# Rounding of the parameters at two points of a step, with temporaries of their own, and the mask placed ahead of a maximum of the next step

## The chip, the cores and the metric

The kernel runs on one core of a Trainium2 chip. Its time is the device time in microseconds (us) of one execution. Before the change the median of three executions is 1976.49 us (1976.48 to 1977.78). The profile is of one more execution, which took 1976.97 us.

## The reference, cut to what matters

```python
# attention: q, k, v are (8, 8, 576, 64)
scores = scale * q @ k.T
kth  = the 32nd largest score of each row
attn = softmax of the scores >= kth, 0 elsewhere
x    = (attn @ v), laid out as (8, 576, 512)
# mixer: U is (576, 32), V (32, 576), w_ch1 (512, 2048), w_ch2 (2048, 512)
u    = x + (x^T @ U @ V)^T
out  = u + relu(u @ w_ch1) @ w_ch2
```

The four mixer parameters arrive as 64-bit numbers. The kernel has to turn each into a rounded 32-bit one itself; the text calls this the rounding.

## The kernel before, in words

**Steps.** Two heads make a pair, four pairs a batch, and there are 32 pairs. A pair's 576 rows are cut into five row tiles, t = 0 to 4. The main loop (L528) runs one step for each row tile, n = 5 * pair + t, 160 steps and two more to drain. Steps with t = 0 to 3 are long (128 rows of two heads, so two chunks of 128x576 scores); those with t = 4 are short (64 rows of each head in one chunk). Twenty steps are one batch.

**What a step issues, in program order.** PE (TensorE) and ACT (ScalarE) work in exactly this order; DVE (VectorE), POOL (GpSimd) and SP (the DMA queue) are ordered by a scheduler.

1. The loads of the next pair on SP (t = 0), and the first maximum of each chunk of step n, on DVE (`first`, L292).
2. Calls of `fill()`, each of which may advance the `mixed` generator and emit a portion of the MLP, with the rest of the transposes of step n-2 between them (`turns`, L334 and L339 on PE, L335 and L340 on ACT) and one transpose of the next pair's q, k (`prep`, L228).
3. `values(n-2)` (L364, L367 or L354) and `scores(n+1)` (L247 on PE, then the copies L265 to L267 or L257 on ACT).
4. The second part of `front(n)`: ACT makes `nmax` (L294) and the exponential of chunk 0 (L272); DVE makes three rounds of match_replace and max for each chunk (L299, L303); for chunk 1 POOL builds the mask from the 32nd value and adds it to the scores (L305, L306); for chunk 0 DVE masks the exponential and sums it (scalar_tensor_tensor, L307, "the mask").
5. Two calls of `fill`, the first transposes of step n-1 (L334), two more calls, and then the exponential of chunk 1 of step n-1 on ACT (L272), which reads what POOL left. Its transposes come first thing in step n+1.
6. `next_params` (L559).

**The MLP.** The MLP of batch b goes into the twenty steps after the batch, in portions of four matmuls: portions of `u @ w_ch1` (L437), each followed by a relu on ACT into a tile `hT` (L447), and portions of `h @ w_ch2` (L454). Every fourth of the latter ends with a sum on DVE (`oT`, L467), whose transposes (L479) and output DMA are emitted with a later portion. `due` is a budget in portions: each `fill` adds `share` in a long step and `SHORT * share` in a short one, and portions are emitted while it is above zero. `mixed(g)` makes `u` for a pair: a transpose of XT (L388), a scaling on DVE (`x`, L390), `pT` (L401), and twice `up` (L413, L415) with its copy to `uT` (L422). The MLP of the first batch is emitted from step 22 on, and that of the last runs behind the loop.

**The rounding.** There are 36 parameter pieces, most of 128x512. `next_params(n)` does three things in this order: it joins every piece that is under way, it splits every piece that was loaded, and it starts n loads. A split is Abs and a conversion of one byte on ACT (L141, L143) with a maximum on POOL between (L142); a join is two bit operations on DVE (L149, L152) and an addition on POOL (L156). `next_params` is called at the end of each step, with 2 in steps 0 and 1, 1 in steps 2 to 17 and 2 from then on. The temporaries `bits` and `low` are taken from the ten buffers of `hT`, two for each piece, five pieces deep; raw pieces have three buffers. `uT`, where u^T of a batch is built, has two buffers of 128x2304, of which the second is first used by batch 1.

Of the kernel before, what the change touches and what calls it, by code (L numbers as in the profile page):

```python
# [8 lines left out]
F32 = mybir.dt.float32  # L9
U8 = mybir.dt.uint8  # L10
U32 = mybir.dt.uint32
# [10 lines left out]
def kernel(  # L22
# [28 lines left out]
    nc = tc.nc  # L51
    B, H, S, D = q.shape
    P = 128
# [3 lines left out]
    NF, NC = F // P, C // P  # L57
# [8 lines left out]
    HT = 10  # L66
# [6 lines left out]
    mlpp = ctx.enter_context(tc.tile_pool(name="mlpp", bufs=2))  # L73
# [9 lines left out]
    WIDE = 2 * P + TAIL  # L83
# [33 lines left out]
    def half(h):  # L117
        return slice(h * D, (h + 1) * D)


    def f64_raw(srcs):


        n, w = srcs[0].shape[0], srcs[0].shape[1]
        raw = mlpp.tile([P, 2 * C], U32, tag="raw", name="raw", bufs=3)[:, 0:w]
        for i, src in enumerate(srcs):
            nc.sync.dma_start(raw[i * n : (i + 1) * n], src)
        return raw[0 : len(srcs) * n]

    def f64_parts(raw):  # L130


        n, w = raw.shape[0], raw.shape[1] // 2
        hi = raw.rearrange("p (w two) -> p w two", two=2)[:, :, 1]
        low8 = raw.bitcast(U8).rearrange("p (w eight) -> p w eight", eight=8)[:, :, 3]
        bits, low = (
            mlpp.tile([P, 2, WIDE], U32, tag="hT", name=name, bufs=HT)
            .rearrange("p a n -> p (a n)")[0:n, 0:w]
            for name in ("bits", "low")
        )  # L140
        nc.scalar.activation(bits.bitcast(F32), hi.bitcast(F32), AF.Abs)  # L141
        nc.gpsimd.tensor_scalar(bits.bitcast(F32), bits.bitcast(F32), TINY, None, ALU.max)  # L142
        nc.scalar.activation(low, low8, AF.Identity, bias=half_bit[0:n], scale=1.0 / 32)  # L143
        return hi, bits, low

    def f64_join(hi, bits, low, outs):


        nc.vector.tensor_scalar(  # L149
            bits, bits, 3, 0x3FFFFFFF, ALU.logical_shift_left, ALU.bitwise_and  # L150
        )
        nc.vector.scalar_tensor_tensor(  # L152
            out=bits, in0=hi, scalar=0xC0000000, in1=bits, op0=ALU.bitwise_and, op1=ALU.bitwise_or
        )
        for dst, form in outs:
            nc.gpsimd.tensor_tensor(dst.bitcast(U32), form(bits), form(low), ALU.add)  # L156

    SLAB = 512

    def same(a):  # L160
        return a
# [9 lines left out]
    for cc in range(NC):  # L171
        for f in range(0, F, SLAB):
            params.append(
                ([moe_w_ch1[cc * P:(cc + 1) * P, 2 * f:2 * (f + SLAB)]], [(w1[:, cc, f:f + SLAB], same)])
            )
# [5 lines left out]
    def next_params(n):  # L181

        while parts:
            f64_join(*parts.pop(0))
        while raws:
            r, outs = raws.pop(0)
            parts.append((*f64_parts(r), outs))
        for _ in range(min(n, len(params))):
            srcs, outs = params.pop()
            raws.append((f64_raw(srcs), outs))  # L190


    raw, qkTs, S2s, uTs, XTs, dens = {}, {}, {}, {}, {}, {}
    probs, PTs = {}, {}

    def load(g):
        b, h0 = g // NPAIR, 2 * (g % NPAIR)
        tiles = []
        ends = loads.tile([P, 2, D], F32, tag="ld_ends", name="ld_ends")
        for name, src in (("q", q), ("k", k)):  # L200
            t = loads.tile([P, NT, 2, D], F32, tag=f"ld_{name}", name=f"ld_{name}")
            for i in range(2):
                nc.sync.dma_start(
                    t[:, :, i, :],
                    src[b, h0 + i, 0:MAIN, :].rearrange("(p t) d -> p t d", t=NT),
                )
            nc.sync.dma_start(
                ends[half(len(tiles))], src[b, h0 : h0 + 2, MAIN:S, :].rearrange("h p d -> p h d")
            )
            tiles.append(t)  # L210
        va, vd, vt = (a[g % NV] for a in (vas, vds, vts))
        for i in range(2):
            nc.sync.dma_start(
                va[:, i], v[b, h0 + i, 0:MAIN, :].rearrange("(p t) d -> p t d", t=NT)
            )
            nc.sync.dma_start(vd[half(i), half(i)], v[b, h0 + i, MAIN:S, :])
        nc.sync.dma_start(vt[TAIL:P], v[b, h0 : h0 + 2, MAIN:S, :].rearrange("h p d -> p h d"))
        raw[g] = tiles, ends
# [51 lines left out]
    def weigh(chunk, E, nmax, total=None):  # L270

        nc.scalar.activation(E, chunk, AF.Exp, bias=nmax, scale=SCALE, accum_out=total)  # L272

    def front(g, t):

        if t == 0:
            dens[g] = small.tile([P, 2 * NT + 1], F32, tag="den", name="den", bufs=3)
        chunks, den = S2s.pop((g, t)), dens[g]  # L280
        n = len(chunks)
        E2 = attn.tile([P, 2 * S], F32, tag="E", name="E", bufs=3)
        Es = [E2[:, c * S : (c + 1) * S] for c in range(n)]
        sums = [den[:, 2 * t + c : 2 * t + c + 1] for c in range(n)]
        probs[g, t] = E2
        curs, ms = list(chunks), [None] * n
        first = small.tile([P, 2, 8], F32, tag="first", name="first", bufs=3)
        nmax = small.tile([P, 2], F32, tag="nmax", name="nmax", bufs=4)
        order = (1, 0) if n == 2 else (0,)
        for c in order:  # L290
            ms[c] = first[:, c]
            nc.vector.max(ms[c], curs[c])  # L292
        yield
        nc.scalar.mul(nmax[:, 0:n], first[:, 0:n, 0], -SCALE)  # L294
        weigh(chunks[0], Es[0], nmax[:, 0:1])
        for i in range(1, TOPK // 8):
            for c in order:
                nxt = attn.tile([P, S], F32, tag="rr", name="rr", bufs=3)
                nc.vector.match_replace(nxt, ms[c], curs[c], NEG)  # L299
                curs[c] = nxt  # L300
            for c in order:
                ms[c] = small.tile([P, 8], F32, tag="m8", name="m8", bufs=8)
                nc.vector.max(ms[c], curs[c])  # L303
        if n == 2:
            nc.gpsimd.tensor_scalar(Es[1], chunks[1], ms[1][:, 7:8], NEG, ALU.is_lt, ALU.mult)  # L305
            nc.gpsimd.tensor_tensor(chunks[1], chunks[1], Es[1], ALU.add)  # L306
        nc.vector.scalar_tensor_tensor(  # L307
            out=Es[0],
            in0=chunks[0],
            scalar=ms[0][:, 7:8],  # L310
            in1=Es[0],
            op0=ALU.is_ge,
            op1=ALU.mult,
            accum_out=sums[0],
        )
        if t == NT:
            del qkTs[g]
        yield
        if n == 2:
            weigh(chunks[1], Es[1], nmax[:, 1:2], sums[1])  # L320
        yield
# [174 lines left out]

    CH = NT + 1
    STEPS = NP * CH
    SLOTS, SHORT = 8, 0.55
    share = MLP_WORK / (NPAIR * SLOTS * (NT + SHORT))  # L500
    fillers, mixing, due = [], [], 0.0

    def fill(n=1):

        nonlocal due
        for _ in range(n):
            if mixing and next(mixing[0], True):
                mixing.pop(0)
            due += share * (SHORT if t == NT else 1)
            while due > 0:  # L510
                if not fillers:
                    due = 0.0
                    break
                done = next(fillers[0], None)
                if done is None:
                    fillers.pop(0)
                else:
                    due -= done

    load(0)  # L520
    next_params(2)
    t = 0
    for _ in prep(0):
        pass
# [3 lines left out]
    for n in range(STEPS + 2):  # L528
        g, t = divmod(n, CH)
        if n < STEPS:  # L530
            if t == 0 and g + 1 < NP:
                load(g + 1)
            if t == 1 and g + 1 < NP:
                ready = prep(g + 1)
            fronts[n] = front(g, t)
            next(fronts[n])
        fill()
        next(turning, None)
        fill()
        next(turning, None)  # L540
        fill()
        next(ready, None)
        fill()
        if n >= 2:
            values(*divmod(n - 2, CH))
        if n + 1 < STEPS:
            scores(*divmod(n + 1, CH))
        if n < STEPS:
            next(fronts[n])
        if n >= 2 and (n - 2) % CH == NT:  # L550
            mixing.append(mixed((n - 2) // CH))
        fill(2)
        if 1 <= n <= STEPS:
            turning = turns(*divmod(n - 1, CH))
        next(turning, None)
        fill(2)
        if 1 <= n <= STEPS:
            next(fronts.pop(n - 1))
        next_params(1 if 2 <= n < 18 else 2)  # L559
    while mixing or fillers:  # L560
        fill()

# [30 lines left out]
```

## Time and profile before

| what | value |
|---|---|
| median of three executions | 1976.49 us |
| profiled execution | 1976.97 us |
| its span, first to last instruction | 1975.2 us |
| PE busy | 1797.4 us (91%) |
| DVE busy | 1640.3 us (83%) |
| ACT busy | 950.5 us (48%) |
| POOL busy | 574.7 us (29%) |
| mean TensorE clock granted | 0.955 of full speed |

Busy time is what the instructions of an engine cover. An idle time stands with the group of instructions that it comes before, and with the engine that ended it. The matmul rows count each float32 matmul twice, since the chip makes two passes, so a portion of four matmuls is a row "x8". The page's second part cuts the span into 40 slices of 49.4 us.

### The profile page before, as it was taken

The page shows a single profiled execution, that of the slowest core. Times are in us where ns is not written, and L with a number is a line of the kernel's source. Part 1 is how long each engine was busy: PE and PEld are TensorE (multiplying, and loading weights), DVE is VectorE, ACT ScalarE, POOL GpSimd, SP SyncE. Part 2 cuts the span into 40 slices and gives each one's busy share as a digit, 9 for nine tenths or more (in the row PEclk, how much of TensorE's full clock was granted, in tenths as well). Part 3 has the DMA queues.
Part 4 walks back from the last instruction along what each step waited for, and adds up shares of the span by engine and source line. Part 5 has one row for each costly group of instructions (what it writes and reads, how often), then busy time and mean ns, then how long its engine had stood idle before and what let it go on. Part 6 is the DMA issues. An engine that isn't in the chain of part 4 may idle for free.

```text
span 1975.2 us, 29361 instructions
## 1 busy us (share of the span) xinstructions
PE 1797.4 (91%) x10656; PEld 1361.2 (69%) x10656; DVE 1640.3 (83%) x3433; ACT 950.5 (48%) x2345; POOL 574.7 (29%) x346
## 2 busy tenths in 40 slices
PE   4666678999999999999999999999999999999999
PEld 2444455777667876677666876677776876678777
DVE  7899998889898988989899888989898898988000
ACT  4555565454554545454554545445454545454111
POOL 4545564222222322222232232222232222223000
PEclk7757689999999999999999999999999999999999
DMA  4212231100001010000101010101001000000000
GB/s 102 72 56 73 66 94 44 29 18 24 15 22 30 19 29 20 24 23 14 25 22 30 20 29 14 26 15 25 24 20 30 22 25 20 15 7 4 8 14 11
DMA packets 121151, 58.22 MB, mean 29 GB/s; under 512 B 89904, under 2 KB 116784, under 8 KB 121008
## 3 DMA queue, kind: packets, MB, share of 16 engines
q1 hardware_dynamic: 121008, 56.36, 10.7%
q8 instruction: 84, 1.38, 0.3%
q14 instruction: 59, 0.48, 0.1%
HBM read 46.89 MB, written 9.44 MB: 29 GB/s over the span
## 4 chain that ended last, share of the span: by engine, by line
PE 75%; DVE 14%; ACT 7%; issue 2%; DMA 1%; POOL 1%; SPq 0%; ACTq 0%; DVEq 0%; POOLq 0%
PE mm L437 24%; PE mm L454 21%; PE sc L247 8%; PE O L367 6%; DVE rr L299 5%; PE tp L334 5%; DVE m L303 5%; ACT E L272 2%; PE O L354 2%; PE up L413 2%; PE up L415 2%; PE O L364 2%; PE tp L228 1%; DVE first L292 1%; DVE E L307 1%
## 5 line engine op out<-in xcount | busy, mean ns | idle before, releaser
L303 DVE MAX8 m<-rr 128x8 f32<-128x576 f32 x864 | 614.7, 747 | 3.6 <-DVE rr L299 0.5
L305 POOL TENSOR_SCALAR E<-Ssb,m 128x576 f32<-128x576 f32 x128 | 284.8, 2225 | 1109.3 <-DVE m L303 728.6
L437 PE MATMUL mm<-uT,w 128*128 128x256 f32 (+1 forms) x2048 | 539.2, 409 | 0.0
L454 PE MATMUL mm<-hT,w 128*128 128x256 f32 (+1 forms) x2048 | 537.1, 408 | 0.0
L437 PEld LDWEIGHTS mm<-uT,w 128*128 128x128 f32 x2048 | 372.3, 190 | 109.3 <-issue 21.9
L454 PEld LDWEIGHTS mm<-hT,w 128*128 128x128 f32 x2048 | 372.1, 190 | 102.0 <-issue 16.6
L299 DVE MATCH_REPLACE8 rr<-m,rr 128x576 f32<-128x576 f32 x576 | 427.7, 743 | 0.0
L292 DVE MAX8 first<-Ssb 128x8 f32<-128x576 f32 x288 | 211.2, 751 | 162.1 <-ACT Ssb L267 160.2
L334 PE MATMUL tp<-ident,E 128*128 128x128 f32 x1152 | 187.3, 287 | 97.2 <-ACT E L272 73.1
L334 PEld LDWEIGHTS tp<-ident,E 128*128 128x128 f32 x1152 | 140.8, 146 | 163.6 <-ACT E L272 95.0
L447 ACT ACTIVATE hT<-mm 128x320 f32<-128x320 f32 (+1 forms) x256 | 105.1, 411 | 273.3 <-PE mm L437 265.5
L335 ACT COPY PT<-tp 128x512 f32<-128x512 f32 x288 | 168.0, 583 | 122.7 <-PE tp L334 119.4
L272 ACT ACTIVATE E<-Ssb,nmax 128x576 f32<-128x576 f32 x288 | 223.3, 775 | 6.9 <-POOL Ssb L306 1.6
L247 PE MATMUL sc<-qkT 64*128 64x288 f32 (+1 forms) x1280 | 212.7, 454 | 0.7 <-ACT qkT L229 0.5
L299 DVE MATCH_REPLACE8 rr<-first,Ssb 128x576 f32<-128x576 f32 x288 | 212.2, 742 | 0.0
L306 POOL TENSOR_TENSOR Ssb<-Ssb,E 128x576 f32<-128x576 f32 x128 | 192.2, 1501 | 10.7
L367 PE MATMUL O<-PT,va 128*64 128x128 f32 x2048 | 151.5, 294 | 0.0
L247 PEld LDWEIGHTS sc<-qkT 64*128 64x128 f32 (+1 forms) x1280 | 111.0, 189 | 52.6 <-issue 26.2
L467 DVE TENSOR_TENSOR oT<-uT,mm 128x320 f32<-128x320 f32 (+1 forms) x64 | 28.3, 442 | 139.2 <-PE mm L454 139.2
L307 DVE SCALAR_TENSOR_TENSOR E<-Ssb,m,E 128x576 f32<-128x576 f32 x160 | 134.0, 838 | 2.5 <-ACT E L272 1.5
L367 PEld LDWEIGHTS O<-PT,va 128*64 128x64 f32 x2048 | 118.6, 145 | 16.9 <-issue 3.1
L376 ACT COPY XT<-O 128x128 f32<-128x128 f32 x128 | 34.1, 267 | 176.5 <-PE O L367 176.5
(64 smaller groups left out, 1426.9 us busy)
## 6 DMA issues: line engine op xcount, KB each, us to landing
raw<-in_moe_w_ch_dram SPq DMA_DIRECT2D x32, 512.0 KB, 3.8
ld_q<-in_q_dram SPq DMA_DIRECT2D x64, 128.0 KB, 2.8
ld_k<-in_k_dram SPq DMA_DIRECT2D x64, 128.0 KB, 2.8
va<-in_v_dram SPq DMA_DIRECT2D x64, 128.0 KB, 2.4
out_dram<-ob SPq DMA_DIRECT2D x64, 128.0 KB, 1.9
ld_ends<-in_q_dram SPq DMA_DIRECT2D x32, 32.0 KB, 2.1
ld_ends<-in_k_dram SPq DMA_DIRECT2D x32, 32.0 KB, 2.1
vd<-in_v_dram SPq DMA_DIRECT2D x64, 16.0 KB, 1.9
```

Source lines behind the costliest of these rows:

```text
L247: nc.tensor.matmul(sc[slice(0, n) if t < NT else half(h), h, 0:HALF], lhsT=qkT[half(h), 0, cols(t)], rhs=qkT[half(h), 1, i * HALF : (i + 1 ...
L272: nc.scalar.activation(E, chunk, AF.Exp, bias=nmax, scale=SCALE, accum_out=total)
L292: nc.vector.max(ms[c], curs[c])
L299: nc.vector.match_replace(nxt, ms[c], curs[c], NEG)
L303: nc.vector.max(ms[c], curs[c])
L305: nc.gpsimd.tensor_scalar(Es[1], chunks[1], ms[1][:, 7:8], NEG, ALU.is_lt, ALU.mult)
L306: nc.gpsimd.tensor_tensor(chunks[1], chunks[1], Es[1], ALU.add)
L334: nc.tensor.transpose(tp[:, j, :], E2[:, a : a + P], ident)
L335: nc.scalar.copy(PT[:, NT * h : NT * h + NT], tp)
L367: nc.tensor.matmul(O[half(h)], lhsT=va[:, h, j, :], rhs=PT[:, NT * h + j], start=False, stop=(j == NT - 1),)
L437: nc.tensor.matmul(ph[:, 0:w], lhsT=w1[:, cc, f * P : (f + 1) * P], rhs=uT[:, cc, lo:hi], start=(cc == 0), stop=(cc == NC - 1),)
L454: nc.tensor.matmul(po[:, 0:w], lhsT=w2[:, f, c * P : (c + 1) * P], rhs=hTs[f][:, 0:w], start=(f == 0), stop=(f == NF - 1),)
```

## The change

Five edits:

- The temporaries of the rounding are four slabs of 128x512 in one `uT` tile that is allocated ahead of all others, so that it takes one of the two buffers. Pieces use the slabs in turn, two slabs each, so two pieces can be under way.
- `next_params(1)` is also called in the middle of each step, between the two `fill` calls ahead of the transposes of step n-1. The call at the end of the step starts one load in even steps and none in odd ones, and the first call, ahead of the loop, starts one in place of two.
- The first of the maxima that step n+1 issues (chunk 1 in long steps) may not stand ahead of the mask of step n on DVE. It is an order in the instruction stream and no semaphore.
- SHORT goes from 0.55 to 0.65, which also lowers `share`.
- `SLAB` is defined further up.

```diff
-        bits, low = (
-            mlpp.tile([P, 2, WIDE], U32, tag="hT", name=name, bufs=HT)
-            .rearrange("p a n -> p (a n)")[0:n, 0:w]
-            for name in ("bits", "low")
-        )
+        if not spare:
+            uT = mlpp.tile([P, NC, S], F32, tag="uT", name="uT")
+            words = uT.rearrange("p c n -> p (c n)").bitcast(U32)
+            spare.extend(words[:, i * SLAB : (i + 1) * SLAB] for i in range(4))
+        bits, low = (spare.pop(0) for _ in range(2))
+        spare.extend((bits, low))
+        bits, low = bits[0:n, 0:w], low[0:n, 0:w]
...
-            nc.vector.max(ms[c], curs[c])
+            ins = nc.vector.max(ms[c], curs[c])
+            if last_mask:
+                tc.add_manual_dep(ins.ins, last_mask.pop(), mybir.DependencyInfo(
+                    mybir.DependencyClass.NoSync, mybir.DependencyReason.DATA
+                ), reason="order")
...
-        nc.vector.scalar_tensor_tensor(
+        ins = nc.vector.scalar_tensor_tensor(
...
+        last_mask.append(ins.ins.name)
...
-    SLOTS, SHORT = 8, 0.55
+    SLOTS, SHORT = 8, 0.65
...
-    next_params(2)
+    next_params(1)
...
-        fill(2)
+        fill()
+        next_params(1)
+        fill()
...
-        next_params(1 if 2 <= n < 18 else 2)
+        next_params((n + 1) % 2)
```

More of the change, by code (lines that the diff above doesn't have):

```diff
@@ L118, in half @@
         return slice(h * D, (h + 1) * D)
+    SLAB = 512
+    spare = []
     def f64_raw(srcs):
@@ L156, in f64_join @@
             nc.gpsimd.tensor_tensor(dst.bitcast(U32), form(bits), form(low), ALU.add)
-    SLAB = 512
     def same(a):
@@ L193 @@
     raw, qkTs, S2s, uTs, XTs, dens = {}, {}, {}, {}, {}, {}
-    probs, PTs = {}, {}
+    probs, PTs, last_mask = {}, {}, []
     def load(g):
```

## The prediction, made before the changed kernel was run

> **What bounds the kernel now.** I read the busy digits first (page, second part).
>
> ```profile
> PE   4666678999999999999999999999999999999999
> ...
> DVE  7899998889898988989899888989898898988000
> ```
>
> For seven slices (some 340 us) PE is half idle while DVE is nearly full; then PE is full, and for the last three DVE has nothing. The steps give the exact borders: step 19's mask starts at 236.55, step 28's score matmuls at 336.56, the last scores end at about 1811. The table by stage (length, then busy us by engine, PE first, DVE third; then the clock granted), its third row one batch:
>
> ```profile
> 11.50:236.55 225.05, 138.97 (x755) 96.41 (x757) 216.12 (x457) 121.18 (x281) 118.72 (x81) 0.67 0.26 72
> 236.55:336.56 100.01, 75.44 (x414) 53.38 (x412) 95.48 (x195) 54.32 (x124) 61.32 (x40) 0.87 0.24 73
> ...
> 470.07:695.06 224.99, 216.33 (x1334) 164.88 (x1332) 200.57 (x420) 113.57 (x284) 59.68 (x32) 1.00 0.09 23
> ```
>
> So up to about 337 us DVE is the bound (96% and 95% busy), from there PE (96%), each batch of twenty steps taking 225.0 us, and the end (163.8 us) is MLP on PE, 158.5 us of it busy. All roundings (L149, last at 322.4) lie in the DVE part. What can be won there is DVE's idle time, in this view of DVE's waits up to 340 us (total, times, longest):
>
> ```profile
> DVE first L292 <- ACT Ssb L267: 17.5, 4, 10.7
> DVE x L390 <- PE tp L388: 6.6, 3, 3.6
> DVE bits L149 <- POOL bits L142: 1.7, 2, 1.5
> ```
>
> 10.65 us of the first row is the wait for the first scores. The rest is 15.2 us: 1.46, 0.75 and 4.65 for scores, 2.04, 3.59 and 0.96 for x, 1.7 for POOL. Up to step 28's first maximum (338.70) DVE's work is the same in both kernels, so what the opening wins or loses is the change of these 15.2 us. In the PE part the gain is in PE's waits of one batch, 8.6 us in all:
>
> ```profile
> PE tp L334 <- ACT E L272: 5.1, 6, 1.3
> ...
> PE tp L479 <- DVE oT L467: 0.7, 1, 0.7
> ```
>
> **The change part by part.** I set the instruction orders of both built programs side by side.
>
> *Rounding twice a step.* It removes and adds no instruction; it starts 1.5 pieces a step throughout. In DVE's order 31 pieces are joined by step 19's mask, where 22 were; all by step 23's, where it was step 27's. Nine joins at 0.42 + 0.68 (L149, L152 undisturbed) move 9.9 us of DVE work ahead of step 19's mask and out of the steps behind it. By itself that is neutral: both sides are DVE's. What it takes away is idle: the hT buffers are no longer lent out. Before, a relu stood 6.8 us behind a join of w (the only L447 wait on POOL), which is what made scores 28 late: the 4.65 us. ACT's four waits for raw pieces (11.0 and 5.2 us) should go too: a raw buffer is freed by the join three pieces earlier, two steps back at 1.5 a step, one and a half at 2. They cost DVE nothing now, as PE and ACT catch up; SP has the same loads, spread out.
>
> *What it adds.* The join now often stands on DVE in the step of its split. Abs waits for the POOL addition of two pieces before (two pieces of slabs), with ACT's copies for the transposes queued behind it; that addition is half a step old, so I cost this at nothing (its ends: 0, and 1.6, the one such wait of before). DVE's first bit operation waits for POOL's maximum, which stands behind POOL's L305 and L306. In step 8 of before these ended at 119.25, 2.3 us after the mask (116.92). In the changed short steps 9 and 19, two joins stand among seven rounds. The first is 4 rounds (2.7 us at 0.667 each, the start-to-start distance of its rounds) behind the mask; its input is ready at 2.3 + 1.3 (addition) + 1.5 (maximum) = 5.1. The second waits 1.5 more. That is 4 us in each of steps 9 and 19, and 1.5 in 4 and 14 by the same count: 11 us. From below it is nothing: before, such waits sum to 1.7 us over 36 joins, and POOL's spans are rough. I take 7, nearer the computed row.
>
> *Mask ahead of the next maximum.* In the order of the changed program one of the two maxima still stands ahead of most masks; the other follows. In the opening this puts step 4's, 9's and 14's mask three rounds (2 us) earlier against the work of the next step, so x, which needs that mask through PE, comes due later on DVE: of the waits for x I keep 1.4 + 0.7 + 1.4 (step 5, 10, 15) in place of 2.04 + 3.59 + 0. The other waits for scores and x (1.46, 0.75, 0.96, 4.65) I count as gone, since PE and ACT no longer stand behind raw pieces and hT, and the 1.7 is replaced by the 7. So idle after is 3.5 + 7 = 10.5, against 15.2: **-4.7**, with ends 3.5 (-11.7) and 14.5 plus up to 3 where PE, at S(28), is as late as DVE (+2.3).
>
> In the PE part, DVE idles 22.6 us a batch waiting for scores, and there the mask now waits for ACT's exponential, which ACT does after the copies: 642.22 first maximum, exponential over at 643.10, mask, second maximum, against two maxima and the mask. DVE goes on 0.3 us later in eight steps of a batch, 0.7 in some; the next wait (1.2 to 4.4 us) takes it back. It shows only where PE waits for DVE: x at step 57 has 0.3 us of room (I take 0.1, ends 0 and 0.3, times 7: +0.7), and oT of step 41, now one maximum (0.67) earlier: 0.4 less of its 0.73 wait, six times: **-2.4**, ends -4.4 and 0.
>
> *SHORT.* Portions shift in four steps of twenty. In 17 one goes behind a transpose (no wait either way). In 2, transposes of oT go behind prep's: a wait of 0.25 becomes about 0.05, six times: -1.1. In 4 a portion moves from the start of the next step to the end of this one. PE's order is unchanged, but ACT now does its relu ahead of the exponential that PE waits for. Both cases are in before, step 43 and step 44:
>
> ```profile
> 523.13 0.44 ACT L447 ACTIVATE hT<-mm 128x320 f32<-128x320 f32 x1 [1.57 <-PE mm L437]
> 523.46 0.77 ACT L272 ACTIVATE E<-Ssb,nmax 128x576 f32<-128x576 f32 x1
> ...
> 524.37 0.66 PE L334 MATMUL tp<-ident,E 128*128 128x128 f32 x4 [1.28 <-ACT E L272]
> ...
> 532.61 0.42 ACT L447 ACTIVATE hT<-mm 128x320 f32<-128x320 f32 x1
> ...
> 532.76 0.66 PE L334 MATMUL tp<-ident,E 128*128 128x128 f32 x4 [0.31 <-ACT E L272]
> ```
>
> In the first the exponential follows a relu and PE's transposes wait 1.28; in the second (exponential at 531.84, relu behind it) they wait 0.31. The second becomes the first: 1.28 - 0.31 = 0.97, seven times: **+6.8**. The end behind the loop holds the same portions: 0.
>
> **Sum.** -4.7 + 0.7 - 2.4 - 1.1 + 6.8 = -0.7 against 1976.97; the median of before is 0.48 below that, so the median predicted is 1975.8. Low ends: -11.7 + 0 - 4.4 - 1.1 + 6.8 = -10.4. High ends: 2.3 + 2.1 + 0 + 0 + 6.8 = +11.2.
>
> **A rule against it.** Three rows, DVE beside POOL:
>
> ```profile
> 228.14 1.40 POOL L306 TENSOR_TENSOR Ssb<-Ssb,E 128x576 f32<-128x576 f32 x1
> 228.36 1.46 DVE L149 TENSOR_SCALAR bits<-bits 128x512 uint32<-128x512 uint32 x1
> ...
> 633.08 0.82 DVE L307 SCALAR_TENSOR_TENSOR E<-Ssb,m,E 128x576 f32<-128x576 f32 x1
> ```
>
> Beside L306 the 0.42 us operation took 1.46; the mask at 633.08 ran beside L305 (631.92, 2.21 long) and took its usual 0.8. The Trainium skill, "SBUF — State Buffer", section "SBUF: two separate sides", has a DVE operation with two SBUF inputs fully blocked while a GpSimd operation that reads SBUF holds the shared ports. By it a mask right behind the last maximum would wait for the end of L305, 2.21 less the 0.67 of that maximum, so an estimated 1.5 us in each long step: 24 us in the sixteen of the opening, and a sum of about +23. The row at 633.08 shows no such wait, and I go by the row.
>
> **Rivals.**
>
> *Faster: the roundings never hold DVE.* Idle after falls to 3.5: -11.7 + 4.0 = -7.7, 1968.8. For it: the 1.7 us of such waits before. Against it: POOL is 53% busy here and works in order.
>
> *Slower: the ordered mask hands its delay to PE.* Place: the wait for the exponential between the two first maxima. Price: 0.3 us in eight steps of 6.6 batches, 16 us if all reaches PE; half of it, with -0.7, gives 1984. It decides from where DVE's lag meets PE's next need without an idle time between, that is in t = 1 and 2, where DVE has no wait at all. Against it: the transposes of chunk 0 need the mask only half a step later.
>
> *It does not do what it says:* only one of two maxima is held, so the order may do nothing; then x keeps its 5.6 us in place of 3.5 and the time is 1978, inside the forecast's band.
>
> **How the numbers follow.** About 0.2% (3.95 us) is what a measurement can tell from no change: faster is below 1972.5, slower above 1980.4. The forecast (gains of the opening paid back in the batches, with the rival that nothing is ordered) gets 0.36, faster 0.33, slower 0.31. The ends of the sum are 1966 and 1988; they leave out the slow rival's far half. The forecast's own range is 1972.5 to 1980.4.
>
> **What would show it.** L447 waits for POOL gone; step 28's scores at 332 (325 in the fast rival); DVE waits for POOL of about 7 us, in steps 4, 9, 14 and 19; a batch of 225.5 us with seven waits of 1.3 before L334 (now L344) in place of six; none of oT above 0.4. A batch under 225 or over 226 makes the prediction wrong in its PE part, scores 28 outside 325 to 339 in its opening.

## The result, and the profile after

The changed kernel takes 1984.57 us (median of four executions, 1984.13 to 1984.73) against 1976.49 us (four, 1974.87 to 1977.78): ratio 1.0041, 95% interval 1.0024 to 1.0058. It is slower by 8.1 us, where no measurable change (1975.8 us) was forecast. The profiled execution of the changed kernel has a span of 1982.4 us, 7.2 us more than before. Of these 7.2 us, 4.0 are there when step 27's mask starts (340.03 before, 344.02 after); up to step 54 0.7 are won back, the five batches from there add 3.5, and the end adds 0.4.

Line numbers move with the edits: the first maximum is L296 (L292 before), the last rounds L308 and L312 (L299, L303), POOL's mask and addition L314 and L315 (L305, L306), the mask on DVE L316 (L307), the bit operations L155 and L158 (L149, L152), POOL's maximum L148 (L142) and its addition of a join L162 (L156). In each experiment the lines are those of its own kernel.

The busy digits of the page, 40 slices, look as before: DVE full for seven slices, then PE.

```profile
PE   4656579999999999999999999999999999999999
...
DVE  7999999989899988989899989989898998888000
```

In the stage table (length; then busy us, PE first and DVE third; clock granted behind POOL) the first two rows end at step 19's mask and at step 28's scores; the third is one batch.

```profile
11.50:255.00 243.50, 146.36 (x761) 100.78 (x757) 234.25 (x470) 129.70 (x296) 138.22 (x96) 0.64 0.29 84
255.00:338.18 83.18, 69.80 (x409) 50.16 (x407) 82.31 (x172) 45.88 (x109) 37.38 (x23) 0.91 0.14 38
473.00:698.65 225.65, 216.35 (x1337) 164.92 (x1332) 202.70 (x421) 113.68 (x284) 58.94 (x32) 1.00 0.09 22
```

Step 28's scores are at 338.18, 1.6 us later than before (336.56), not at 332. A batch takes 225.65 us instead of 225.0. Both stages have lost.

DVE's waits in the opening (total, times, longest) are nevertheless shorter than before:

```profile
DVE first L296 <- ACT Ssb L271: 10.3, 1, 10.3
DVE uT L155 <- POOL uT L148: 5.9, 4, 1.6
DVE x L400 <- PE tp L398: 2.5, 2, 1.3
```

Without the first wait, which only starts the work, that is 8.4 us against 15.2: 6.8 us won. So DVE's work must have grown. The groups of the bit operations, first before (up to 340 us), then after (up to 344), with busy us and mean ns behind the bar, show by how much:

```profile
L152 DVE SCALAR_TENSOR_TENSOR bits<-raw,bits 128x512 uint32<-128x512 uint32 (+3 forms) x36 | 25.8, 716 | 0.1
L149 DVE TENSOR_SCALAR bits<-bits 128x512 uint32<-128x512 uint32 (+3 forms) x36 | 18.9, 525 | 1.7 <-POOL bits L142 1.7
```

```profile
L158 DVE SCALAR_TENSOR_TENSOR uT<-raw,uT 128x512 uint32<-128x512 uint32 (+3 forms) x36 | 31.3, 868 | 0.0
L155 DVE TENSOR_SCALAR uT<-uT 128x512 uint32<-128x512 uint32 (+3 forms) x36 | 21.5, 597 | 6.3 <-POOL uT L148 5.9
```

The same 72 instructions take 52.8 us instead of 44.7: 8.1 us more. That is not all. At the border that the prediction named, step 28's first maximum, DVE is 4.7 us later (338.70 before, 343.36 after). Counted from the start of each DVE instruction to the start of the next, up to there, bit operations take 7.9 us more, rounds and first maxima 3.7 (they follow each other less closely) and the small operations on `den` 1.0, while the masks take 0.8 less and idle time is 7.1 less (0.3 of it in the first wait). Step 28's scores, only 1.6 us late, do not measure this: before, DVE waited 4.65 us for them, and after, it comes to them without a wait.

Where the bit operations lose their time is seen in the timelines of POOL and DVE around step 16's mask (start, duration, engine):

```profile
216.47 2.22 POOL L314 TENSOR_SCALAR E<-Ssb,m 128x576 f32<-128x576 f32 x1 [3.66 <-DVE m L312]
218.78 1.41 POOL L315 TENSOR_TENSOR Ssb<-Ssb,E 128x576 f32<-128x576 f32 x1
```

```profile
216.87 0.62 DVE L155 TENSOR_SCALAR uT<-uT 128x512 uint32<-128x512 uint32 x1
217.41 0.81 DVE L316 SCALAR_TENSOR_TENSOR E<-Ssb,m,E 128x576 f32<-128x576 f32 x1
...
218.15 0.75 DVE L296 MAX8 first<-Ssb 128x8 f32<-128x576 f32 x1
218.82 1.91 DVE L158 SCALAR_TENSOR_TENSOR uT<-raw,uT 128x512 uint32<-128x512 uint32 x1
```

L158, 0.68 us where nothing stands beside it, begins just after POOL's addition and lasts until 220.73, half a microsecond behind that addition's end; the text calls this being held. Six L158 of 1.9 us and four L155 of 1.53 (alone 0.42) are in the opening, each beside L315, and one L155 of 128x32 of 1.22; before, five bit operations took over 1 us. The maximum at 218.15 is the one that the order holds behind the mask. If it did not stand there, the bit operation would begin 0.67 us earlier, at 218.15, ahead of the addition; a pair of runs below has both cases.

In the batches, PE's waits of one batch show the one that the prediction priced, 6.1 us where it was 5.1; oT has hardly moved (0.7 before):

```profile
PE tp L344 <- ACT E L276: 6.1, 6, 1.3
...
PE tp L489 <- DVE oT L477: 0.6, 1, 0.6
```

### The profile page after: what moved, and what is told of

It reads as the page before. It is cut to its first block, busy times and chain, and to the rows that moved or that the text cites. A ratio compares the mean times of both kernels' runs of the same rounds, so it can differ in the third digit from the quotient of the medians.

```text
span 1982.4 us, 29370 instructions
## 1 busy us (share of the span) xinstructions
PE 1799.6 (91%) x10656; PEld 1362.8 (69%) x10656; DVE 1663.4 (84%) x3433; ACT 951.4 (48%) x2345; POOL 567.6 (29%) x346
## 3 DMA queue, kind: packets, MB, share of 16 engines
q1 hardware_dynamic: 121008, 56.36, 10.7%
## 4 chain that ended last, share of the span: by engine, by line
PE 75%; DVE 15%; ACT 6%; issue 2%; POOL 2%; DMA 0%; SPq 0%; DVEq 0%; ACTq 0%; POOLq 0%
PE mm L447 25%; PE mm L464 20%; PE sc L251 8%; DVE rr L308 6%; PE O L377 6%; PE tp L344 5%; DVE m L312 5%; ACT E L276 2%; PE O L364 2%; PE up L423 2%; PE up L425 2%; PE O L374 1%; DVE first L296 1%; DVE E L316 1%; PE tp L232 1%
## 5 line engine op out<-in xcount | busy, mean ns | idle before, releaser
L312 DVE MAX8 m<-rr 128x8 f32<-128x576 f32 x864 | 615.9, 747 | 4.6
L314 POOL TENSOR_SCALAR E<-Ssb,m 128x576 f32<-128x576 f32 x128 | 283.8, 2217 | 1150.8 <-DVE m L312 833.2
L464 PEld LDWEIGHTS mm<-hT,w 128*128 128x128 f32 x2048 | 372.1, 190 | 102.0 <-issue 16.6
L308 DVE MATCH_REPLACE8 rr<-m,rr 128x576 f32<-128x576 f32 x576 | 427.3, 742 | 0.0
L296 DVE MAX8 first<-Ssb 128x8 f32<-128x576 f32 x288 | 215.5, 753 | 117.9 <-ACT Ssb L271 117.9
L457 ACT ACTIVATE hT<-mm 128x320 f32<-128x320 f32 (+1 forms) x256 | 105.2, 411 | 277.5 <-PE mm L447 276.5
L308 DVE MATCH_REPLACE8 rr<-first,Ssb 128x576 f32<-128x576 f32 x288 | 212.1, 742 | 0.0
L315 POOL TENSOR_TENSOR Ssb<-Ssb,E 128x576 f32<-128x576 f32 x128 | 186.4, 1456 | 10.7
L316 DVE SCALAR_TENSOR_TENSOR E<-Ssb,m,E 128x576 f32<-128x576 f32 x160 | 130.3, 815 | 25.8 <-ACT E L276 18.6
```

Of the source, the lines that this page charges most:

```text
L296: ins = nc.vector.max(ms[c], curs[c])
L464: nc.tensor.matmul(po[:, 0:w], lhsT=w2[:, f, c * P : (c + 1) * P], rhs=hTs[f][:, 0:w], start=(f == 0), stop=(f == NF - 1),)
```

## The experiments

Two checkpoints are used: the start of step 27's mask, by which all roundings are done (340.03 us before), and the mean batch from the masks of step 54 to 154 (five batches; 224.99 us before). "Long" counts bit operations on 128x512 of over 1 us. Ratios are against the kernel before, timed beside each run.

| kernel | median us | ratio (95%) | mask 27 | batch | long |
|---|---|---|---|---|---|
| before | 1976.49 | 1 | 340.03 | 224.99 | 5 |
| after | 1984.57 | 1.0041 (1.0024-1.0058) | 344.02 | 225.68 | 10 |
| short_alone | 1974.38 | 0.9992 (0.9983-1.0001) | 333.38 | 225.74 | 6 |
| after_short_055 | 1980.26 | 1.0020 (1.0011-1.0029) | 343.49 | 224.94 | 10 |
| after_no_order | 1981.37 | 1.0027 (1.0015-1.0038) | 338.82 | 225.74 | 7 |
| order_alone | 1987.27 | 1.0058 (1.0045-1.0071) | 352.01 | 225.03 | 5 |
| twice_alone | 1964.94 | 0.9946 (0.9934-0.9958) | 330.37 | 224.99 | 7 |
| middle_call_earlier | 1996.08 | 1.0103 (1.0090-1.0116) | 354.62 | 225.63 | 8 |
| addition_in_halves | 1982.31 | 1.0035 (1.0022-1.0048) | 342.14 | 225.69 | 5 |
| short_065_to_step_27 | 1978.29 | 1.0009 (1.0001-1.0017) | 335.11 | 226.06 | 4 |
| twice_and_order | 1979.73 | 1.0018 (1.0009-1.0027) | 343.96 | 224.88 | 10 |
| twice_and_slabs | 1975.66 | 1.0005 (0.9996-1.0014) | 340.05 | 224.99 | 9 |
| twice_and_short | 1969.03 | 0.9962 (0.9948-0.9976) | 329.71 | 225.72 | 6 |
| twice_and_halves | 1966.06 | 0.9947 (0.9934-0.9959) | 331.09 | 224.98 | 5 |
| order_short_steps | 1964.77 | 0.9942 (0.9930-0.9954) | 329.23 | 224.81 | 6 |
| order_long_steps | 1971.18 | 0.9970 (0.9959-0.9980) | 337.40 | 224.66 | 11 |

### SHORT by itself

**short_alone**, on the kernel before, and **after_short_055**, on the changed kernel:

```diff
-    SLOTS, SHORT = 8, 0.55
+    SLOTS, SHORT = 8, 0.65
```

```diff
-    SLOTS, SHORT = 8, 0.65
+    SLOTS, SHORT = 8, 0.55
```

> The kernel before with SHORT 0.65 and nothing else changed. Theory (SHORT puts the relu ahead of the exponential in step 44 of each batch): the opening is as before, step 28's scores at 336.6; a batch takes 225.0 + 0.97 - 0.18 = 225.8 us, with one more PE wait of about 1.3 us before the first transposes of E; 6.6 batches give +5, so about 1981.8 us, ratio 1.0027. Rival (SHORT is neutral and the batches of the changed kernel lose by the ordered mask): batch 225.0, time 1976.5, ratio 1.0000.

> The changed kernel with SHORT back at 0.55. Theory: step 28's scores stay at 338.2, since SHORT acts from step 22 on; a batch takes 225.6 - 0.8 = 224.8 us, the wait of 1.28 in the step after the short one falls to 0.3; time 1984.6 - 5.3 = 1979.3 us, ratio 1.0014. Rival (the ordered mask is what the batches pay): batch stays at 225.6 and the time at 1984.6, ratio 1.0041.

The batches answer as the theory has it in both: 0.75 us longer with 0.65, 0.74 shorter without. But short_alone is not slower than before, since it also wins 6.7 us by mask 27. What goes there is this wait of ACT, in the timeline of the kernel before:

```profile
325.95 0.44 ACT L447 ACTIVATE hT<-mm 128x320 f32<-128x320 f32 x1 [6.75 <-POOL w L156]
```

With other portions in steps 24 to 27 no relu in short_alone waits for a join. I had counted this gain to the new temporaries alone. In the changed kernel that wait is gone already, so SHORT only costs there: 4.3 us (1984.57 against 1980.26). The rival for the batches (the ordered mask pays) falls: the batch of after_short_055, with the order, is 224.94.

### The order taken away, and the order alone

**after_no_order**, on the changed kernel:

```diff
-        last_mask.append(ins.ins.name)
```

**order_alone**: the kernel before with the change's lines for `last_mask`, nothing else.

> The changed kernel without the order of mask and maximum; rounding twice a step in its own slabs and SHORT 0.65 stay. Theory (the order puts a first maximum between the last rounds and the second bit operation, which then begins 2.57 us behind chunk 1's last maximum, beside POOL's addition, where it took 1.91 us; without the order it begins at 1.91 us and is over before the addition): bit operations of over 1.2 us fall from ten to about four, DVE's bit operations lose 7 us, the waits for x come back with up to 4, step 28's scores at 335, time about 1981 us, ratio 1.0023. Rival (the crowding of two advances a step lengthens them, wherever the mask stands): ten long bit operations stay, the waits for x come back, scores at 341 and time 1987, ratio 1.0053.

> The kernel before with the order of mask and maximum and nothing else. Theory (order costs only where it shifts bit operations beside POOL's addition): by the built order three or four of them fall there against five in the kernel before, so the opening is -1 to -4 (waits for x shorter): step 28's scores at 333 to 336; a batch 0 to 0.4 below 225.0, as x and oT come earlier; time 1972 to 1976 us, ratio 0.998 to 1.000. Rival (the wait of the mask for the exponential reaches PE): batch 225.4 or more, time 1979 or more, ratio over 1.001.

Without the order the changed kernel has seven long bit operations instead of ten, and 42.5 us of bit operations by mask 27 instead of 52.8; it is 3.2 us faster, as expected. But it stays slower than the kernel before, for a reason found below. The order alone is much dearer than either theory had it: +11 us, and all of it in the opening, with five long bit operations as before. DVE's waits in its opening say where:

```profile
DVE bits L149 <- POOL bits L142: 11.8, 14, 3.3
DVE first L292 <- ACT Ssb L267: 11.2, 2, 10.4
DVE x L395 <- PE tp L393: 10.0, 5, 3.6
```

14 waits for POOL's maximum in place of two. ACT makes `nmax` from the first maxima, then the exponential, and only then comes Abs of the next piece, in its fixed order. ACT's waits of `nmax` for `first` are 41.1 us in this opening (14.6 before), so Abs and POOL's maximum come later, while the order built for DVE has the bit operation right behind them (POOL's maximum 218.26 to 219.75, the bit operation at 219.79). The waits are not the whole cost: of the 12.7 us by which step 28's first maximum is later (351.35), idle time is 7.2, and 4.9 are rounds and first maxima that follow each other less closely. Batches are not touched (225.03).

### The rounding twice a step by itself

**twice_alone**: the kernel before with the changed calls of the rounding, temporaries still borrowed from `hT`, no order, SHORT 0.55.

```diff
-    next_params(2)
+    next_params(1)
...
-        fill(2)
+        fill()
+        next_params(1)
+        fill()
...
-        next_params(1 if 2 <= n < 18 else 2)
+        next_params((n + 1) % 2)
```

> The kernel before with the rounding advanced twice a step (the calls of the changed kernel), temporaries still borrowed from hT, no order, SHORT 0.55. Theory (the twice-a-step calls cost what the changed kernel without the order shows, 7 us of DVE waits for POOL, and have the long wait of the relu for a join gone, as all joins are over by step 23): the mask of step 27 near 339, as without the order, batch 225.0, time 1976 us, ratio 1.000. Rival (the slabs, two pieces deep, are what holds the rounding in the changed kernel: Abs waits for the addition of two pieces before): mask of step 27 at 334, time 1971 us, ratio 0.997.

The rival holds, and more: 1964.94 us, 11 us faster than before. DVE's waits in its opening:

```profile
DVE first L292 <- ACT Ssb L267: 10.5, 1, 10.5
DVE x L390 <- PE tp L388: 5.3, 3, 2.2
```

No wait for POOL is left. Idle time behind the first wait is 5.3 us, 9.9 less than before, and mask 27 is 9.7 us earlier. Everything else that the change does takes this gain away. Three kernels add the rest one at a time.

**twice_and_order** adds the lines for `last_mask`; **twice_and_slabs** adds the four slabs in the idle uT tile; **twice_and_short** sets SHORT to 0.65.

> twice_alone (rounding twice a step, temporaries from hT, SHORT 0.55; 1964.9 us) with the order of mask and maximum. Theory (the order moves the first maxima behind the mask, so ACT's exponential and all behind it come later, bit operations stand right behind POOL's maximum and beside its addition): DVE waits for POOL from 0 to 6 or more, long bit operations from 7 to about 10, mask of step 27 from 330.4 to 341 or later, time about 1976 us, ratio 1.000. Rival (the order costs only with the once-a-step calls or only with the two-piece slabs): mask of step 27 at 330 to 333, time 1965 to 1967 us, ratio 0.995.

> twice_alone with the temporaries in four slabs of the idle uT buffer (two pieces deep in place of five), no order, SHORT 0.55. Theory (Abs of a piece waits for POOL's addition of the piece two before, with ACT's other work queued behind it): ACT waits of some 29 us for additions in ten places, DVE waits for POOL 7 to 8 us, mask of step 27 at 338 to 339 as without the order, time 1976.4 us, ratio 1.000. Rival (SHORT 0.65 was what held the opening of the changed kernel without the order): mask of step 27 at 330 to 332, time 1965 to 1966 us, ratio 0.995.

> twice_alone with SHORT 0.65. Theory (SHORT takes away only the relu's wait for a join, which twice_alone no longer has, and costs 0.75 us a batch): mask of step 27 at 330.4, batch 225.75, time 1964.9 + 5 = 1970 us, ratio 0.997. Rival (SHORT helps the opening by itself): mask of step 27 at 324 to 327, time 1963 to 1965 us, ratio 0.994.

All three first theories hold in their mechanism; the order is dearer than expected (1979.73 us, not 1976). It brings the ten long bit operations and DVE's waits for POOL, those of the changed kernel:

```profile
DVE first L292 <- ACT Ssb L267: 10.6, 1, 10.6
DVE bits L149 <- POOL bits L142: 5.9, 4, 1.6
DVE x L395 <- PE tp L393: 2.1, 2, 1.0
```

Up to step 28's first maximum (329.05 and 343.30, +14.3) the account from DVE's starts closes: second bit operation +6.4, idle +2.7, rounds and first maxima +4.5 (they follow each other less closely), `den` +1.0, the others -0.3. How the order lengthens the second bit operation is seen behind step 13's mask, first in twice_alone, then in twice_and_order:

```profile
174.32 0.81 DVE L307 SCALAR_TENSOR_TENSOR E<-Ssb,m,E 128x576 f32<-128x576 f32 x1
...
175.06 0.68 DVE L152 SCALAR_TENSOR_TENSOR bits<-raw,bits 128x512 uint32<-128x512 uint32 x1
...
175.69 1.40 POOL L306 TENSOR_TENSOR Ssb<-Ssb,E 128x576 f32<-128x576 f32 x1
```

```profile
181.11 0.81 DVE L311 SCALAR_TENSOR_TENSOR E<-Ssb,m,E 128x576 f32<-128x576 f32 x1
...
181.84 0.75 DVE L292 MAX8 first<-Ssb 128x8 f32<-128x576 f32 x1
...
182.47 1.40 POOL L310 TENSOR_TENSOR Ssb<-Ssb,E 128x576 f32<-128x576 f32 x1
182.52 1.90 DVE L152 SCALAR_TENSOR_TENSOR bits<-raw,bits 128x512 uint32<-128x512 uint32 x1
```

Without the order the bit operation begins 0.63 us ahead of POOL's addition and keeps its 0.68 us, although the addition begins while it runs; seven L152 of twice_alone stand so. With the order a first maximum comes between, the bit operation begins 0.05 us behind the start of the addition, and it takes 1.90; six L152 of twice_and_order stand so.

The slabs without the order cost 10.7 us by the medians (1964.94 to 1975.66), by ACT's waits in the opening of twice_and_slabs:

```profile
ACT XT L382 <- PE O L373: 39.0, 21, 2.8
ACT uT L147 <- POOL w L162: 29.3, 10, 5.1
```

Abs of a piece waits for the addition of the piece two before; in twice_alone, with temporaries borrowed from `hT` and five pieces deep, no Abs waits for an addition. Behind Abs stand ACT's copies, and DVE then waits for POOL in three places (5.7 us). In after_no_order, which is twice_and_slabs with SHORT 0.65, the same row is 29.0 us in ten waits: that is why it stays slow. With the order, the row is gone (2.4 us for the parameter U alone). Whether joins stand earlier there, or ACT, which then waits 35.9 us for first maxima, only comes later itself, was not separated. after_short_055, which is twice_and_order plus slabs, is 0.5 us from it. So the costs of the order (14.8) and of the slabs (10.7) do not add: each hides the other.

### In which steps the order costs

**order_short_steps** and **order_long_steps**, on twice_and_order:

```diff
-        last_mask.append(ins.ins.name)
+        if t == NT:
+            last_mask.append(ins.ins.name)
```

```diff
-        last_mask.append(ins.ins.name)
+        if t < NT:
+            last_mask.append(ins.ins.name)
```

> twice_alone with the order for the masks of short steps (t = 4) only. Theory (in a short step the rounds of its one chunk depend on each other, and the order takes out what stood between them, so they stand 0.80 apart in place of 0.67 and the bit operations come before POOL's maximum is ready): DVE waits for POOL 5 to 6 us, long bit operations about 7 as in twice_alone, mask of step 27 at 338 to 340, time 1973 us, ratio 0.9985. Rival (the order costs in the long steps alone): mask of step 27 at 330 to 332, time 1965 us, ratio 0.9945.

> twice_alone with the order for the masks of long steps (t = 0 to 3) only. Theory (there the order moves bit operations beside POOL's addition and nothing else of weight): long bit operations ten or more, bit operations 52 us in place of 46, DVE waits for POOL under 2 us, mask of step 27 at 336 to 337, time 1971 us, ratio 0.9975. Rival (the order costs in the short steps alone): mask of step 27 at 330 to 332, time 1965 us, ratio 0.9945.

Long steps: 11 long bit operations, bit operations 51.8 us by mask 27 (46.2 in twice_alone), waits for POOL 2.3, mask 27 7.0 us later, 1971.18 us: the theory, with its numbers. Short steps: the theory falls, mask 27 is 1.1 us earlier and the time that of twice_alone. Yet both together cost 13.6 us at mask 27, 7.7 more than the two alone add up to. What comes only then is seen in the timeline of DVE in step 9, a short one, of twice_and_order:

```profile
123.28 0.76 DVE L307 MAX8 m<-rr 128x8 f32<-128x576 f32 x1
125.61 0.43 DVE L149 TENSOR_SCALAR bits<-bits 128x512 uint32<-128x512 uint32 x1 [1.57 <-POOL bits L142]
...
128.15 0.74 DVE L303 MATCH_REPLACE8 rr<-m,rr 128x576 f32<-128x576 f32 x1
130.26 0.43 DVE L149 TENSOR_SCALAR bits<-bits 128x512 uint32<-128x512 uint32 x1 [1.37 <-POOL bits L142]
```

Two bit operations stand in front of rounds and wait for POOL. In order_long_steps and in twice_alone the next step's first maxima stand between the rounds of a short step. The waits are the smaller part: from order_long_steps to twice_and_order step 28's first maximum comes 6.6 us later (336.74 and 343.30), of which idle time is 1.7, rounds and first maxima 3.1, `den` 1.0 and bit operations 0.9. That both places must be ordered for this to appear is what the runs show; why the built order of order_short_steps escapes it (its waits for POOL are 1.7 us in two places) was not followed further.

### The hold beside POOL's addition

**addition_in_halves**, on the changed kernel, and **twice_and_halves**, the same edit on twice_alone:

```diff
-            nc.gpsimd.tensor_tensor(chunks[1], chunks[1], Es[1], ALU.add)
+            for a0, a1 in ((0, S // 2), (S // 2, S)):
+                nc.gpsimd.tensor_tensor(
+                    chunks[1][:, a0:a1], chunks[1][:, a0:a1], Es[1][:, a0:a1], ALU.add
+                )
```

> The changed kernel with POOL's addition of chunk 1's mask (128x576, 1.40 us) as two additions of 288 columns each. Theory (DVE is held until POOL's instruction ends): the longest bit operations fall from 1.9 and 1.53 us to about 1.3 and 1.0, ten of them lose 5 to 6 us together, step 28's scores at 333, time 1979 us, ratio 1.0013. Rival (it is the share of the memory that POOL takes, whatever its instructions): bit operations as long as before, time 1984.6 us, ratio 1.0041.

> twice_alone with POOL's addition of chunk 1's mask in two halves of 288 columns. Theory (DVE is held until the POOL instruction ends, so a half holds it for less; no DVE wait for POOL is there that a later POOL could lengthen): the seven bit operations of over 1.2 us become one or none, bit operations 46.2 to 42 or 43 us, mask of step 27 at 327 to 328, time 1962 us, ratio 0.993. Rival (one more POOL instruction a step makes DVE wait for POOL's maximum, as it did in the changed kernel, 5.9 to 11.1 us): mask of step 27 at 331 to 334, time 1966 to 1969 us, ratio 0.996.

The place behind step 16's mask, on POOL and DVE, in addition_in_halves:

```profile
217.21 2.00 POOL L316 TENSOR_TENSOR Ssb<-Ssb,E 128x288 f32<-128x288 f32 x2
```

```profile
217.25 1.29 DVE L158 SCALAR_TENSOR_TENSOR uT<-raw,uT 128x512 uint32<-128x512 uint32 x1
```

L158 takes 1.29 us instead of 1.91: it is held by 0.61 us instead of 1.23, and ends half a microsecond behind the first half (218.00) and not behind the second (219.21). So the hold goes by the POOL instruction, as the theory has it, and bit operations fall from 52.8 to 45.5 us. It also works the other way: the second half, which begins while L158 runs, takes 1.25 us where halves take 0.80, and so the two take 2.00 here; the median of all 128 pairs is 1.55, against 1.41 in one piece. DVE's waits for POOL's maximum rise from 5.9 to 11.1 us, and only 2.3 us of the time is won. On twice_alone, with fewer holds to shorten, it wins nothing (46.2 to 44.9 us of bit operations, 1.3 us of new waits for POOL): 0.9947 against 0.9946.

**middle_call_earlier**, on the changed kernel, tried the opposite, more bit operations beside the addition:

```diff
+        next_params(1)
         if n < STEPS:
             next(fronts[n])
...
-        fill()
-        next_params(1)
-        fill()
+        fill(2)
```

> The changed kernel with the call in the middle of the step moved ahead of the second part of front(n), so that POOL's maximum stands ahead of chunk 1's mask. By the built order 15 to 18 bit operations begin in the time in which POOL adds chunk 1's mask, against 10 to 12. Theory (a bit operation beside POOL's two-input addition is held until the addition ends, 1.2 us each): 15 or more of over 1.2 us, +6 to +9 us on DVE, less up to 5.9 of waits for POOL that go: mask of step 19 0 to 5 us later, time 1984 to 1989 us, ratio 1.004 to 1.006. Rival (long bit operations come of POOL's queue, which holds fewer at this place): fewer than ten long ones, no waits for POOL, time 1973 us, ratio 0.998.

Both expectations fail. Eight long bit operations, fewer than after, and yet 11.5 us slower, since DVE's waits for POOL's maximum are 16.6 us in 11 places. Counting in the built order which bit operations fall beside the addition did not foresee this run: the waits shift DVE against POOL, and the count takes them as none.

### SHORT in the opening only

**short_065_to_step_27**, on the kernel before:

```diff
-            due += share * (SHORT if t == NT else 1)
+            short = 0.65 if n < 28 else SHORT
+            due += MLP_WORK / (NPAIR * SLOTS * (NT + short)) * (short if t == NT else 1)
```

> The kernel before with SHORT 0.65 up to step 27 and 0.55 from step 28 on; nothing else changed. Theory (short_alone won 6.7 us by the mask of step 27, since portions shift and the relu that waited 6.75 us for a join no longer comes behind it, and paid 0.75 in each batch): mask of step 27 at 333.4, batch 225.0, time 1970 us, ratio 0.9967. Rival (the gain is given back in batch 1, where the portions fall back to their old places): batch 1 longer by 3 or more, time 1974 us, ratio 0.9987.

The opening wins 4.9 us, but four of the five batches then take 225.7 us, and the other, with a granted clock of 0.99 in place of 1.00, 227.33. PE's waits of a batch, in all five, now have

```profile
PE tp L479 <- DVE oT L467: 2.0, 2, 1.8
```

where it was 0.7. Both expectations are wrong: the loss is in every batch, not in batch 1 alone. That `due` carries its shifted phase on from the opening would explain it, and is not shown.

## Why the prediction was wrong, step by step

**The step that failed** is the first one of the working: "DVE's work is the same in both kernels, so what the opening wins or loses is the change of these 15.2 us". The instructions are the same, but not the time they take: up to step 28's first maximum bit operations take 7.9 us more, rounds and first maxima 3.7 and `den` 1.0, with the masks 0.8 less. So the opening, forecast at -4.7, came out at +4.7 there, although idle time fell by more than forecast. twice_and_order beside twice_alone shows that it is the order that lengthens DVE's work. The prediction itself showed the row that says how, L149 at 228.36 with 1.46 us beside L306, and then used it only to judge the mask. It did not ask which other DVE operations the changed order puts beside L306. The order of the built program could have pointed there: in step 16 the second bit operation begins 0.04 us behind the start of POOL's addition (218.82 and 218.78), with a maximum just ahead of it that takes 0.67. It is no sure method, since the same count failed for middle_call_earlier.

Neither sign that was set for the opening and the batches showed the miss: step 28's scores at 338.18 lie inside 325 to 339, and the batch inside 225 to 226. The scores were the wrong place to look, since DVE's lag is 4.7 us where theirs is 1.6.

**The idle time** was forecast well: 10.5 against 8.4 measured. POOL's waits were put at 7 and are 5.9, in steps 9 and 19 alone, two each; the waits for x, put at 3.5, are 2.5. The relu's wait for POOL is gone as forecast, and no L457 waits for a join.

**Abs at nothing** (ends 0 and 1.6) came true in the changed kernel (2.4 us, U alone), but for another reason than given. "That addition is half a step old" does not hold without the order: ten waits, 29 us. What the slabs cost was hidden by the order, so this term came out by luck.

**The order in the PE part** (x +0.7, oT -2.4) is about nothing: batches with it and SHORT 0.55 are 224.94 and 225.03 against 224.99, and the wait for oT went from 0.7 to 0.6, not to 0.33. **SHORT** (+6.8 and -1.1, where six times 0.2 would be 1.2) was right in mechanism and a little dear: 1.0 us more of PE's wait for the exponential in a batch (still in six places, not seven), 0.75 us of its time, 4.3 us in all. The batch of 225.5 was measured as 225.65.

**The rule against it.** The mask beside POOL's one-input operation (L314) keeps its 0.81 us, as the row at 633.08 said; no 1.5 us for each mask, and no 24 in all. The Trainium skill, "SBUF — State Buffer", section "SBUF: two separate sides", has the loser of a lock fully blocked for the other's whole instruction: beside POOL's two-input addition the runs agree (1.91 for 0.68, and 1.29 when the addition is cut in two); beside its one-input operation they do not (0.81 for the mask, 0.87 for L158). The rule was wrong for the operation that I priced with it and right for L158, which I did not price. One input or two on POOL's side is not all of it either: beside POOL's maximum (L148, one input) six masks of after_no_order take about 1.16 us, though none is held to its end.

**The rivals.** The fast one, "the roundings never hold DVE", is what rounding twice a step does by itself: no DVE wait for POOL, and 1964.94 us where it said 1968.8. The slow one named the order and 1984 us, which is close to the number by chance: its place and price are refuted, since no batch pays for the order; it costs in the opening. The third, that the order may do nothing, falls too: on twice_alone the order costs 14.8 us.

Where the time came from, added one edit at a time along one path, each median less that of the kernel before beside it: rounding twice -11.2, order to +3.5 (14.7), slabs to +3.9 (0.5), SHORT to +8.1 (4.1). Along another path the slabs come second and cost 10.6, SHORT 5.7, and the order last 3.0. Of the edits only the first was worth having. Rounding twice a step, alone or with the order in short steps, beats both kernels: 1964.94 and 1964.77 us, ratio 0.9946 and 0.9942, no difference between the two that could be told.

## What to carry to other kernels

Where one engine bounds a stage, do not take its work as fixed because its instructions are the same: list which of them take longer beside which instruction of another engine, and look in the built order for what an edit moves there. An order that is added for one pair of instructions moves everything that a scheduler places around them, and is tried alone. Edits made together can hide both a gain and each other's costs, so a bundle that comes out even is to be taken apart before it is judged.

## What the runs showed of the hardware

- A bit operation on DVE that begins beside POOL's two-input addition ends 0.3 to 0.6 us behind that instruction: on 128x512 it takes 1.91 us instead of 0.68, or 1.53 instead of 0.42, and one on 128x32 took 1.22 instead of 0.17. One that begins 0.63 us ahead of the addition keeps its 0.68. Beside POOL's mask, of one input, it is 0.87 and 0.62. The maxima and match_replaces are not held: on average 0.75 and 0.74 us with the addition beside them (151 and 129 in the changed kernel), as without.
- POOL's addition of 128x576 takes 1.41 us, two of 128x288 together 1.55 (medians of 128). A half that begins while a bit operation of two inputs runs on DVE takes 1.25 us instead of 0.80.
- In a short step with nothing between its rounds a maximum starts 0.77 us behind its match_replace, and the next match_replace 0.87 us behind that; where two chunks take turns it is 0.66 and 0.72 (twice_and_order). So a short step is dearer for DVE when nothing stands between its rounds.
